# A fused attention and gated feed-forward kernel: three weight loads go to ScalarE's queue, scores wait for half of K, and the written-out order is replaced

## Chip, core and metric

The kernel runs on one core of a Trainium2 chip. The metric is the device time of one execution in microseconds (us). Before the change it is 263.43 us, the median of three runs (263.19 to 264.03).

## What is computed

From the reference, cut to what matters (one batch, 2048 tokens, width 512, 32 heads of 16, four segments of 512 tokens, feed-forward width 1792):

```python
q, k, v = x @ wq, x @ wk, x @ wv            # split into 32 heads, 4 segments
for s in range(4):
    p = softmax(q[s] @ k[s].T * scale + causal_mask)
    a_dot = p @ v[s]
    pq = phi(q[s])                           # t + 1 if t > 0 else exp(t)
    a_mem = (pq @ M) / (pq @ z + 1e-6)
    out[s] = g_head * a_mem + (1 - g_head) * a_dot
    M, z = M + phi(k[s]).T @ v[s], z + phi(k[s]).sum(rows)
a = concat(out) @ wo
b = (relu(x @ W_gate) * (x @ W_up)) @ W_down
result = g * a + (1 - g) * b                 # g = sigmoid(x . gate_w), one per token
```

## The kernel before

**Work.** Each segment's attention is done in four units of eight heads. A unit has four score groups (`qk`, line 634, eight matmuls each), each followed on ScalarE by one exponential of 128x2048 values from PSUM to SBUF (line 656), by masking on GpSimd (line 685), and, when all four are done, by the product with V (line 707). The score groups all write the same four PSUM banks, so a score group waits for the exponential of the one before it. Every second unit has a further group for the diagonal blocks (line 647). Between two score groups TensorE is given matmuls of 512 columns from other parts, here called fills: the projections of q, k and v (weights `wq_sb`, `wk_sb`, `wv_sb`), the two feed-forward projections (`wg_sb`, `wu_sb`) and the output (`wd_sb`, `wo_sb`). All go through `full`: as one matmul (line 476), or, when TensorE is in its column form already, as four quarter-width ones (line 480).

**After a projection.** Q is copied from PSUM by VectorE (line 567). K is copied to `ktr` (line 583), and then masked into `KT` in three pieces (line 586): the first serves score groups with `r = 0`, the second those with `r = 1`, the third the diagonal. `ktr` also goes through an exponential on ScalarE (line 546) and two VectorE steps to `pkT` (lines 541 and 542).

**Order.** Nothing is scheduled at run time. Every step is a task with an engine and with the tasks it depends on; `ORDER` lists the tasks' numbers in the order in which they are written out, and `UNITS` says which PSUM bank or buffer each takes. Each engine executes its own tasks in that order; the waits between engines come from the dependences.

**Loads.** Loads at the start stand in the code ahead of the plan. ScalarE's queue issues the second quarter of the first x rows (n1) and one row block of wq (q1), then ScalarE loads its table and copies two pieces of x. SyncE's queue issues, in this order: n0, q0, a transposed half of x, q2, q3, wk in two halves of rows, wv, the first 512 columns of W_gate (g0) and of W_up (u0), gate_w, beta, the next 512 columns of W_gate and W_up (g1, u1), the rest of the first x rows (n2), the transposed x of the second segment, and the remaining columns. In the built program every load adds to one of eight landing counters, taken in turn, and waits, before it is issued, until the earlier load on its counter has landed.

Of the kernel before, what the change touches and what calls it, by code (L numbers as in the profile page):

```python
# [9 lines left out]
ACT = mybir.ActivationFunctionType  # L10
# [83 lines left out]
"""  # L94

UNITS = (
    "456701237654305000122212611232212100100000100000000130110000003000300002301130200031220202"
    "14113320353207112630381119110d320b102a221c100102102200031022000121112200033220200104563012"
    "000003200000002201100000320002000020011312212203031113a32230207013430163028200b21350219122"
    "c303d0112011031320210001131302032220322331021456721030000023000000022011000002300020000310"  # L100
    "111220213112163223212b3012121530243008013a01390037612d201c00121201322100312122323022013100"
    "145631200000023000000023011000000000000007001131230220103122362025300b320220081234211a0239"
    "715d4027326c10011200110"
)


class Slot:


    def __init__(self, cands):  # L110
        self.cands, self.units, self.left = tuple(cands), (), 0

    @property
# [66 lines left out]
def kernel(  # L180
# [74 lines left out]
    def work():  # L255
        return plan.one("ps", range(7, -1, -1))


    LANDS = dict(n0=3470, n1=3600, q0=4500, q1=4550, x0=5600, q2=5900, q3=6400, ka=7700,
                 kb=9600, v=11000, g0=12500, u0=13800, gw=14800, be=15100, g1=16300, u1=17500,  # L260
                 n2=18500, x1=21500, g2=22800, u2=23900, g3=25000, u3=26100)

# [726 lines left out]
```

## Time and profile before

| | |
|---|---|
| median of three runs | 263.43 us |
| the profiled execution's own time | 263.58 us |
| its span | 261.9 us |
| TensorE clock granted | 1.0 throughout |
| TensorE matmul busy | 254.7 us (97%) |
| VectorE busy | 203.7 us (78%) |
| ScalarE busy | 183.2 us (70%) |
| GpSimd busy | 64.2 us (25%) |
| DMA, mean rate over the span | 75 GB/s |
| DMA, rate in the first six slices of 6.5 us | 193, 293, 292, 269, 221, 241 GB/s |

The span is what the profiler saw of the program; the profiled execution's time is 1.7 us longer. Engine rows are named PE (TensorE matmul), PEld (TensorE weight load), DVE (VectorE), ACT (ScalarE), POOL (GpSimd) and SP (SyncE); a q behind the name (SPq, ACTq) is that engine's issue of a load. L476 is line 476 of the kernel. A row of the timeline reads: start in us, duration in us, engine, line, operation, what is written from what, shapes, count, and in brackets the idle time of the engine just before it with what ended it. A row of the list of waits reads: who waited for whom, total us, times, longest. A row of the chain of waits reads: start, duration, what the chain ran through. A row by stretch reads: the stretch, its length, then busy us and count of PE, PEld, DVE, ACT and POOL, the TensorE clock, the busy share of the DMA engines, and GB/s.

### The profile page before, as it was taken

Reading aid. Unit: us, or ns where it says so; the run is one execution under the profiler, and the core shown is the slowest. Engines: PE = TensorE matmul, PEld = TensorE weight load, DVE = VectorE, ACT = ScalarE, POOL = GpSimd, SP = SyncE. Lnnn points to the kernel's source line nnn. Section 1 sums busy time; section 2 is a strip of 40 time slices with the busy share of each in tenths; the row PEclk is TensorE's granted clock in tenths of the full one; section 3 lists DMA queues with packets and bytes.
Section 4 is the critical chain, followed back from the end, with each engine's and each line's share of the span. In section 5 each row is a group of like instructions: output and inputs, shape, how many; then the busy total and the mean of one; then the engine's idle time right before and its main releaser. Section 6 shows DMA issues by size and latency. Waiting matters only on the chain.

```text
span 261.9 us, 8759 instructions
## 1 busy us (share of the span) xinstructions
PE 254.7 (97%) x3769; PEld 116.9 (45%) x3798; DVE 203.7 (78%) x472; ACT 183.2 (70%) x168; POOL 64.2 (25%) x168
## 2 busy tenths in 40 slices
PE   8899999999999999999999999999999999999995
PEld 3344434453444354544444444445444444445454
DVE  1899999888896756958989868858988678788622
ACT  2199998998877788787768576878486768972100
POOL 8023462313321223222112222122122232120000
PEclk9999999999999999999999999999999999999999
DMA  7999887021411202100210500140200100330011
GB/s 193 293 292 269 221 241 145 4 43 23 84 34 43 92 22 72 45 0 3 83 21 3 95 4 21 55 150 3 80 4 20 32 7 23 97 108 3 3 43 40
DMA packets 31581, 19.71 MB, mean 75 GB/s; under 512 B 16056, under 2 KB 30008, under 8 KB 31544
## 3 DMA queue, kind: packets, MB, share of 16 engines
q1 hardware_dynamic: 31128, 18.90, 27.1%
q8 instruction: 29, 0.48, 0.7%
q10 hardware_dynamic: 416, 0.26, 0.3%
q14 instruction: 8, 0.07, 0.1%
HBM read 13.21 MB, written 2.55 MB: 60 GB/s over the span
## 4 chain that ended last, share of the span: by engine, by line
PE 90%; DVE 5%; issue 1%; DMA 1%; SPq 1%; ACT 0%; DVEq 0%; ACTq 0%
PE ps L476 54%; PE ps L480 19%; PE ps L634 8%; PE ps L707 7%; DMA wq_sb<-in_A_wq_dram 1%; DVE ktr L583 1%; PE ps L647 1%; DVE KT L586 1%; PE ps L827 1%; SPq L304 1%; DVE QT L567 0%; PE ps L763 0%; DVE T L738 0%; DVE hT L877 0%; PE ps L803 0%
## 5 line engine op out<-in xcount | busy, mean ns | idle before, releaser
L656 ACT ACTIVATE E<-ps 128x2048 bf16<-128x2048 f32 x64 | 120.1, 1877 | 32.7 <-PE ps L634 22.5
L685 POOL TENSOR_SCALAR_AFFINE_SELECT E<-E 128x256 bf16<-128x256 bf16 x128 | 55.5, 458 | 170.3 <-ACT E L656 170.3
L877 DVE TENSOR_TENSOR hT<-ps,rgr 128x512 bf16<-128x512 f32 x56 | 37.8, 683 | 13.1 <-PE ps L476 8.4
L476 PE MATMUL ps<-xT,wu_sb 128*128 128x512 bf16 x163 | 45.6, 380 | 0.7 <-issue 0.5
L871 ACT ACTIVATE rgr<-ps 128x512 bf16<-128x512 f32 x56 | 32.6, 596 | 15.3 <-PE ps L480 8.2
L476 PE MATMUL ps<-wd_sb,hT 128*128 128x512 bf16 (+1 forms) x174 | 41.7, 354 | 0.6 <-issue 0.5
L476 PE MATMUL ps<-xT,wg_sb 128*128 128x512 bf16 x149 | 40.9, 380 | 0.3
L738 DVE STREAM_TRANSPOSE T<-ps 128x512 f32<-128x512 f32 x32 | 22.2, 705 | 6.7 <-PE ps L707 6.6
L634 PE MATMUL ps<-QT,KT 32*128 32x320 bf16 (+3 forms) x512 | 25.4, 273 | 0.3
L476 PEld LDWEIGHTS <-wu_sb 128*128 128x128 bf16 x170 | 15.3, 98 | 19.4 <-issue 3.0
L476 PEld LDWEIGHTS <-hT 128*128 128x128 bf16 x178 | 15.6, 98 | 17.6 <-issue 2.1
L903 DVE TENSOR_SCALAR osr<-ps,ngcol 128x512 bf16<-128x512 f32 (+2 forms) x18 | 12.3, 691 | 13.3 <-PE ps L480 9.1
L476 PEld LDWEIGHTS <-wg_sb 128*128 128x128 bf16 x156 | 14.3, 98 | 17.8 <-issue 2.1
L707 PE MATMUL ps<-E,Vp 128*17 128x320 bf16 (+3 forms) x512 | 19.4, 273 | 0.0
L634 PEld LDWEIGHTS <-KT 32*128 32x128 bf16 x512 | 7.6, 92 | 25.7 <-issue 24.6
L656 ACT ACTIVATE Em<-ps 128x2048 bf16<-128x2048 f32 x8 | 15.0, 1874 | 5.0 <-PE ps L647 5.0
L480 PE MATMUL ps<-xT,wg_sb 128*32 128x512 bf16 x272 | 17.8, 379 | 0.0
L476 PE MATMUL ps<-wv_sb,xT 128*128 128x512 bf16 x59 | 16.7, 380 | 0.8 <-DMA wv_sb<-in_A_wv_dram 0.6
L480 PE MATMUL ps<-wd_sb,hT 128*32 128x512 bf16 (+1 forms) x296 | 16.9, 359 | 0.0
L476 PE MATMUL ps<-xT,wq_sb 128*128 128x512 bf16 x57 | 15.8, 380 | 0.4 <-ACT xT L528 0.2
L476 PE MATMUL ps<-xT,wk_sb 128*128 128x512 bf16 x54 | 15.3, 379 | 0.2 <-issue 0.2
L480 PE MATMUL ps<-xT,wu_sb 128*32 128x512 bf16 x216 | 15.0, 379 | 0.0
(100 smaller groups left out, 293.1 us busy)
## 6 DMA issues: line engine op xcount, KB each, us to landing
out_dram<-osr SPq DMA_DIRECT2D x15, 128.0 KB
wd_sb<-in_B_W_down_dram SPq DMA_DIRECT2D x2, 896.0 KB
xn<-in_A_x_dram SPq DMA_DIRECT2D x3, 512.0 KB
cdr<-coefs SPq DMA_DIRECT2D x6, 256.0 KB
xn<-coefs SPq DMA_DIRECT2D x6, 256.0 KB
wg_sb<-in_B_W_gate_dram SPq DMA_DIRECT2D x2, 512.0 KB
wu_sb<-in_B_W_up_dram SPq DMA_DIRECT2D x2, 512.0 KB
wg_sb<-in_B_W_gate_dram SPq DMA_DIRECT2D x2, 384.0 KB
```

Source lines behind the costliest of these rows:

```text
L304: nc.sync.dma_start_transpose(out=xT[0][:, NC // 2:NC, :], in_=x[0:L, halves[1]])
L476: nc.tensor.matmul(out, lhsT=lhsT, rhs=rhs, start=start, stop=stop)
L480: nc.tensor.matmul(out[r], lhsT=lhsT[:, r], rhs=rhs, start=start, stop=stop, tile_position=(0, 32 * j))
L583: d = plan.add("DVE", 600, key - RQK, lambda: nc.vector.tensor_copy(ktr[ks.i][:], bank(sl)), [a], DVL + 40, need=[ks], frees=[sl])
L634: nc.tensor.matmul(ps[:, j * L + o:j * L + o + L - q], lhsT=KT[i][rows, kb, 3 * r:3 * r + 2].rearrange("p h q -> p (h q)"), rhs=QT[i][rows ...
L656: last_exp[0] = [plan.add("ACT", 66 + 4 * L / 1.2, key, lambda: nc.scalar.activation(dst, ps[:, 0:4 * L], ACT.Exp, scale=SCALE), [a] + war ...
L685: nc.gpsimd.affine_select(out=m[:, :, o:o + HP], in_=m[:, :, o:o + HP], compare_op=ALU.is_ge, fill=0.0, base=HP, pattern=[[0, 4], [1, HP]] ...
L707: nc.tensor.matmul(bank(sl)[32 * m:32 * m + HW, q:q + w], lhsT=(Vp[i] if n < 4 else Vm)[:, kb, r, 4 * c + j, 0:HW], rhs=rhs, start=(n == 0 ...
L738: done.append(plan.add("DVE", 633, key - RL, lambda r=r, sl=sl: nc.vector.transpose(T[ts.i][:, r], bank(sl)), [a] + done, 75 if r else 0, ...
L871: r = plan.add("ACT", 478, key - RL, lambda sl=gsl, rs=rs: nc.scalar.activation(rgr[rs.i][:], bank(sl), ACT.Relu), [g], ACL, frees=[gsl])
L877: nc.vector.tensor_tensor(hT[hs1.i][:], bank(sl), rgr[rs.i][:], ALU.mult)),
L903: nc.vector.tensor_scalar(osr[os.i][:, n0 - c0:n1 - c0], bank(sl)[:, 0:n1 - n0], ngcol[:, tt:tt + 1], None, ALU.mult)),
```

## The change

The second row half of wk, the second row half of wv, and u0 are no longer issued by SyncE ahead of the plan. They become three tasks on ScalarE that stand in its order after its two copies of x, chained one behind the other. SyncE keeps the first halves of wk and wv, then g0, gate_w, beta, g1, u1 and the rest as they were.

A score group now depends on its own masked piece of K (`prj["k", seg, c][r]`) instead of on all three.

`ORDER` and `UNITS` are new throughout, since the number of tasks and the assumed landing times (`LANDS`) changed. In the new order the first score group stands behind 30 wide matmuls from line 476 (34 before), the second to fifth behind two fewer than before, and from the eighth to the thirty-seventh group the counts are equal. On VectorE the product for the first `pkT` stands ahead of the third copy of K. Among SyncE's later loads wo now goes ahead of the transposed x of the third segment and of W_down.

```diff
-    got_k = [load_rows(nc.sync, wk_sb, A_wk, i, "k") for i in range(2)]
-    got_v = load_cols(nc.sync, wv_sb, A_wv, 0, D, "v")
-    load_gu(0)
+    got_k = [load_rows(nc.sync, wk_sb, A_wk, 0, "k")]
+    got_v = [load_rows(nc.sync, wv_sb, A_wv, 0, "v")]
+    got_g[0] = load_cols(nc.sync, wg_sb, B_W_gate, *FP[0], "g0")
     nc.sync.dma_start(out=gwb[:], in_=gate_w.partition_broadcast(P))
...
-        a = matmuls(key, xin(seg) + [got_v] + war, sl, [
+        a = matmuls(key, xin(seg) + got_v + war, sl, [
...
-            e = score(key, lambda r=r, k=k: qk(u, r, k), [prj["q", seg, c]] + prj["k", seg, c],
+            e = score(key, lambda r=r, k=k: qk(u, r, k), [prj["q", seg, c], prj["k", seg, c][r]],
                       Ef[:], eread.get(n - RE, []))
...
     got_x[0] = x0_tasks()
+
+    def rows(w, ap):
+        return lambda: nc.scalar.dma_start(out=w[:, 2:4, :],
+                                           in_=ap.rearrange("(c p) n -> p c n", p=P)[:, 2:4, :])
+    deps = got_x[0][0]
+    for got, emit, lat in (
+            (got_k, rows(wk_sb, A_wk), 2600), (got_v, rows(wv_sb, A_wv), 4300),
+            (got_u, lambda: nc.scalar.dma_start(
+                out=wu_sb[:, :, 0:FP[0][1]],
+                in_=B_W_up.rearrange("(c p) n -> p c n", p=P)[:, :, 0:FP[0][1]]), 6800)):
+        a = plan.add("ACT", 470, K(-8), emit, deps, lat)
+        if got is got_u:
+            got_u[0] = a
+        else:
+            got.append(a)
+        deps = [(a, 0.0)]
     load_late()
```

More of the change, by code (lines that the diff above doesn't have):

```diff
@@ L30 @@
 ORDER = """
[63 rows of a table removed]
[63 rows of a table added]
 """
 UNITS = (
[L97 to L103, printed above, removed]
+    "456701237654305000102222211131222123100000110000000120110000030000000002301100101021023210"
+    "24310332350007011621082209121d201a213b203c001112000130031110213231032112102032301145671320"
+    "000003200000002201100000130003000001011322201203031213b22132227303431061238021a30150029201"
+    "c000d1102011030212230021122211022320332323031245610320000031000000023011000002200010000200"
+    "11023131301222110b0235303311380114201a300611291207123d021c12000211122000102132223121323021"
+    "345632010000021000000023011000003300000000701122353021013021122026302b2233302a221411080117"
+    "105d610c223901101200110"
 )
@@ L256, in work @@
         return plan.one("ps", range(7, -1, -1))
-    LANDS = dict(n0=3470, n1=3600, q0=4500, q1=4550, x0=5600, q2=5900, q3=6400, ka=7700,
-                 kb=9600, v=11000, g0=12500, u0=13800, gw=14800, be=15100, g1=16300, u1=17500,
-                 n2=18500, x1=21500, g2=22800, u2=23900, g3=25000, u3=26100)
+    LANDS = dict(n0=3470, n1=3500, q0=4200, q1=4500, x0=5500, q2=6050, q3=6650, ka=7600,
+                 va=9800, g0=12600, gw=13800, be=14300, g1=15600, u1=17000, n2=18100, x1=21200,
+                 g2=22500, u2=23600, g3=24700, u3=25800)
     def arrival(name):
@@ L322 @@
     got_d, got_o = [], []
-    plan.add("SP", 22000, -1e9, None, xfer=4500.0)
+    plan.add("SP", 21000, -1e9, None, xfer=4500.0)
     def load_late():
```

126 rows, old and new, of the table ORDER are left out of this document.

## The prediction

> **What bounds the kernel now.** I read the page's busy times first, then the chain of waits, the list of waits in the first 40 us, the timeline of the opening, and the DMA rate by microsecond.
>
> ```profile
> PE 254.7 (97%) x3769; PEld 116.9 (45%) x3798; DVE 203.7 (78%) x472; ACT 183.2 (70%) x168; POOL 64.2 (25%) x168
> ```
>
> TensorE works 254.7 of 261.9 us. What a change of order and of loads can win lies in the few microseconds where TensorE does not work; the chain shows where they are:
>
> ```profile
> 3.19 3.19 DMA wq_sb<-in_A_wq_dram
> 6.43 3.64 PE ps L476 x16
> ...
> 12.91 0.40 PE ps L634 x8
> 13.31 2.26 PE ps L476 x10
> 15.57 0.33 PE ps L634 x8
> 15.90 2.69 PE ps L476 x12
> 18.60 0.33 PE ps L634 x8
> ```
>
> From 12.91 us on a score group (L634, eight matmuls) and the projections between two of them (L476) follow each other without a hole, and this goes on to 259 us. Ten fills between two scores make a period of 2.60 us (12.91 to 15.51 in the timeline), twelve make 3.02 us (15.51 to 18.53), so a 512-wide fill costs 0.216 us. Before 12.91 the list of waits has one TensorE wait that the change can reach:
>
> ```profile
> PE ps L476 <- DMA wv_sb<-in_A_wv_dram: 0.6, 1, 0.6
> ```
>
> From the end of the last wk matmul to the first wv matmul at 11.51 the hole in starts is 0.757 us more than the usual 0.216. That is the most that can be won here: 0.76 us, 0.3% of the time. (The short gap at 12.77 is a missing matmul record: six weight loads stand beside five matmuls.) The timeline shows ScalarE beside it:
>
> ```profile
> 4.03 0.65 ACT L528 CAST xT<-ps 128x256 bf16<-128x256 f32 x2 [0.88 <-PE ps L513]
> ...
> 10.82 1.23 ACT L546 ACTIVATE ex<-ktr 128x512 bf16<-128x512 bf16 x2 [6.14 <-DVE ktr L583]
> ...
> 13.37 1.88 ACT L656 ACTIVATE E<-ps 128x2048 bf16<-128x2048 f32 x1 [1.32 <-PE ps L634]
> ...
> 16.14 1.88 ACT L656 ACTIVATE E<-ps 128x2048 bf16<-128x2048 f32 x1
> ```
>
> ScalarE is free from 4.68 to 10.82 us, then does two exponentials of K (0.52 us apart) and the first score's exponential, 1.88 us, which the second score group waits for. From there ScalarE is over 90% busy up to 40 us, so a late start is not made up.
>
> The trace also records when the sixteen parts of each load report. The last parts: n0 3.31 us, n1 (ScalarE's queue) 3.51, q3 6.80, first half of wk 7.67, second half 8.40, wv 11.47, g0 (first part of W_gate) 12.90, u0 (first part of W_up) 14.26, gate_w 14.71. In KB landed since the start: 1280 at 7.67, 1536 at 8.40, 2048 at 11.47, 2560 at 12.90, 3072 at 14.26, 3200 at 14.71. I call this the landing curve.
>
> **The change, part by part.** *Three issues on ScalarE.* The two it has now took 0.48 and 0.53 us (0.80 to 1.84), and its table load starts only at 1.87: its stream is served in order. Three more cost 1.5 us, free in the idle stretch if nothing holds them. But the changed program's listing gives each load one of eight landing counters in turn, and a load waits until the earlier load on its counter has landed. SyncE's loads wait so too, and hold nothing else. On ScalarE the second half of wk waits for q3, that of wv for the first half of wv, and u0 for gate_w, which stands on SyncE's queue behind g0. Behind u0 stand the first exponential of K and all that follows.
>
> *Gate 1, second half of wk.* It starts at 6.85 (q3 at 6.80), not at 4.76 as on SyncE. TensorE does six wq, two wk and one wq matmul from 6.43, 9 x 0.216, and stands at 8.38. When does the half land? At best as n0, start to landing 2.50 us: 9.35. By the curve, with nothing of g0 ahead of it (1280 + 256 + 256 = 1792 KB), 9.93. If it takes turns with g0, of which some 100 KB are ahead, 1536 + 100 + 512 = 2148 KB, 11.75. After all of g0, 12.2. That the two queues are served side by side is seen at the start, where n0 and n1 land 0.2 us apart. I take 10.9, about midway between 9.93 and 11.75, because the slow parts of wv (9.19 to 11.47) need not fall on it. After it come 11 wq and wk matmuls and two of wv (2.8 us), the change of form (0.1), the first score and twelve fills (3.02): second score at landing + 5.93 = 16.83.
>
> *Gate 2, ScalarE.* gate_w is now behind 2176 KB at least (n, wq, x, half wk, half wv, g0, itself): 11.83 by the curve; with both second halves before it, 2688 KB, 13.25. I take 13.2, the second halves being issued by 9 us. Then the issue of u0 (0.05 + 0.5), two exponentials (1.0), the first score's (1.88) and 0.1: second score at landing + 3.55 = 16.75. On VectorE the product pkT, now ahead of the third copy of K, waits for the same first exponential; after it come 0.35, 0.27 and 0.61 us and then four W_gate fills, at landing + 3.4: just covered by gate 2. u0 itself then lands near 16.8 (as n1, 2.7 us, with 0.3 for its size), needed at 17.2: covered by 0.4 us, and a loss one for one past that.
>
> *What it is compared with.* Before the second to fifth scores the new order has two fills less (42 against 44 at the second), from the eighth on the same number. The point of the old run that answers is 15.51 - 2 x 0.216 = 15.08. The later gate, 16.83, is 1.75 us behind, and nothing later gives it back: TensorE has no hole after 13 us to fill. Bounds: gates at 9.93 and 11.83 give 15.86, +0.8; at 12.2 and 13.35 they give 18.13, +3.05; at the least row, 9.35, gate 1 gives +0.2.
>
> *Score waits for its own half of K.* The first score needed three masked pieces of K, done at 12.1, while TensorE was on wv until 12.9: the wait cost nothing. Now the first piece is due at landing + 2.3, TensorE at landing + 2.9: 0.6 us of cover.
>
> *SyncE.* Two issues leave it (0.47 and 0.51 us) and one is halved. Its loads up to u0 were all issued by 6.84, before their bytes had their turn, so this wins nothing. Of the reordered later loads W_down landed by 42.9 and is first used at 68.7, 26 us of cover. *Rest of the order.* 36 quarter matmuls (L480, 54 ns apart) become 9 whole ones of 216 ns: no difference. Changes of matmul form number 152 against 151, some 0.1 us each.
>
> The Trainium skill, "DMA: Bandwidth & Descriptors", section "Issuing engines are not separate DMA queues", says that loads of all engines run on the same sixteen DMA engines and that issuing from several saves only issue time. The landings above agree: wk was issued 2.9 us and u0 7.4 us before it landed, so issue time was not what they waited for. By that rule the split brings none of the rate that the second rival below needs, and I set its chance lower for it.
>
> The sum against the profiled execution: 263.58 + 1.75 = 265.3, of which 261.9 was the span and 1.7 lies around it. That execution is 0.15 above the median of 263.43; for the median I predict 265.2.
>
> **The rivals.** *A longer hold on ScalarE.* SyncE's later issues took much longer than 0.5 us when much was queued:
>
> ```profile
> 9.10 1.91 SPq L267 DMA_DIRECT2D wu_sb<-in_B_W_up_dram  x1
> ```
>
> If u0's issue takes 1.91 on ScalarE, gate 2 becomes 13.2 + 4.96 = 18.16, +3.1: 266.5. Against it: ScalarE's own queue has only two small loads before u0.
>
> *The two queues fill the idle DMA time (not slower).* The mean rate sagged where wv was under way:
>
> ```profile
> 8.00:9.00 1.00, 1.00 (x6) 0.44 (x5) 1.00 (x3) 0.00 (x0) 0.00 (x0) 1.00 0.71 219
> ...
> 11.00:12.00 1.00, 0.49 (x3) 0.25 (x4) 1.00 (x4) 1.00 (x2) 0.00 (x0) 1.00 1.03 365
> ```
>
> At 365 GB/s from 7.67 the 1152 KB up to gate_w (half wv, g0, gate_w, second half of wk) would be in by 10.9, and gate 2 (14.45) would not bind. Gate 1 decides: at its least of 9.35 the second score comes at 15.28, +0.2, the same time, 263.6. To be level it would have to land at 9.15, 2.3 us after its issue, when no load of the opening took less than 2.5; with every hold gone, -0.76 (262.7) is the end.
>
> *Only the first piece of the hold.* Both gates at their low curve values: 264.2, on the border of what can be measured.
>
> **How the numbers follow.** About 0.3%, 0.8 us, is what a measurement of this kernel can tell from no change. Both gates near the values taken (+0.9 to +2.6): 0.62. Longer hold or later landing (over +2.6): 0.17. Low curve values: 0.12, half of it counted as slower by over 0.3%. Idle DMA time filled: 0.09, of which 0.03 faster by more than 0.3% (all of the hole won, and a little of the run's own spread), the rest the same. So slower 0.62 + 0.17 + 0.06 = 0.85, same 0.12, faster 0.03. The range, 263.7 to 266.6, leaves out about 0.1 at either end.
>
> **What would show it.** Right: in the profile after, ScalarE's third new issue starts with gate_w's landing, near 13 us, with the first exponentials of K behind it near 14; TensorE waits for wk_sb from about 8.4 to 11; the second score starts near 16.8; no TensorE hole from 20 us on. Step by step wrong: first exponential of K before 12 us (gate 2 does not bind); wk_sb wait under 1 us (gate 1 sized wrongly); holes past 20 us (the loss is in the new order instead). The forecast is wrong if the second score group starts before 15.5 us.

## The result, and the profile after

The changed kernel takes 277.67 us (median of five, 275.0 to 278.45), the kernel before 263.43 (262.97 to 264.03) beside it: ratio 1.0525, 95% interval 1.0469 to 1.0580. The prediction was 265.2, with a range up to 266.6. The direction was right; the loss is 14.2 us instead of 1.75. The traced execution of the changed kernel took 277.82 us, with a span of 276.1 against 261.9.

The page first, busy times and the row of the granted TensorE clock in 40 slices (6.9 us each; 9 is full):

```profile
PE 260.3 (94%) x3742; PEld 119.4 (43%) x3771; DVE 204.5 (74%) x472; ACT 183.9 (67%) x168; POOL 62.5 (23%) x168
...
PEclk9868699999999999999999999999999999999999
```

TensorE is busy 5.6 us longer for the same work, and its clock row, which held 9 throughout before, has two dips, an 8 and a 6 in slices 2 and 3 and again in slices 4 and 5. So there are two losses: time in which TensorE stands still, and time in which it works slowly. The list of waits in the first 40 us gives the standstill (total us, times, longest):

```profile
PE ps L476 <- DMA wk_sb<-in_A_wk_dram: 5.4, 1, 5.4
PE ps L476 <- DMA wu_sb<-in_B_W_up_dram: 3.8, 1, 3.8
```

Before, the one wait of this kind was 0.6 us for wv; it is gone. Now TensorE waits once for the second half of wk and once for u0, two of the three loads that went to ScalarE. The rows by stretch give the slow work (length, busy us of PE, PEld, DVE, ACT, POOL, then the clock, the DMA share and GB/s):

```profile
10.00:20.00 10.00, 5.68 (x22) 2.02 (x24) 4.02 (x9) 1.42 (x3) 0.00 (x0) 0.66 1.13 229
20.00:30.00 10.00, 6.24 (x28) 2.27 (x28) 4.03 (x11) 5.31 (x6) 1.57 (x4) 0.79 1.24 234
```

A mean clock of 0.66 over 10 us, where it is either 1.0 or 0.5, is (1 - 0.66) x 10 / 0.5 = 6.8 us at half clock. The clock records put two such stretches of 6.83 us at 12.07 to 18.89 and at 25.72 to 32.55. They begin 3.3 and 2.9 us after TensorE stopped (8.76 and 22.82), while it still stands, and last into the work behind the hole. The timeline shows what led to it, and what it cost:

```profile
6.50 0.38 ACTq L928 DMA_DIRECT2D wk_sb<-in_A_wk_dram  x1
...
8.47 0.38 ACTq L928 DMA_DIRECT2D wv_sb<-in_A_wv_dram  x1
...
11.12 8.29 SPq L274 DMA_TRANSPOSE xT<-in_A_x_dram  x1
...
13.21 0.38 ACTq L933 DMA_DIRECT2D wu_sb<-in_B_W_up_dram  x1
...
14.16 1.03 PE L476 MATMUL ps<-xT,wk_sb 128*128 128x512 bf16 x2 [5.39 <-DMA wk_sb<-in_A_wk_dram]
...
15.41 3.61 PE L476 MATMUL ps<-xT,wk_sb 128*128 128x512 bf16 x8
...
15.95 0.63 ACT L546 ACTIVATE ex<-ktr 128x512 bf16<-128x512 bf16 x1 [10.93 <-DVE ktr L583]
...
22.42 0.40 PE L634 MATMUL ps<-QT,KT 32*128 32x448 bf16 x8
...
26.57 1.89 PE L476 MATMUL ps<-xT,wu_sb 128*128 128x512 bf16 x4 [3.76 <-DMA wu_sb<-in_B_W_up_dram]
```

The second half of wk is issued by ScalarE at 6.50, right behind q3's landing (6.48 in this trace), and lands at 14.11, 7.6 us later. u0 is issued at 13.21, right behind gate_w's landing (13.19), and lands at 26.53, 13.3 us later. Eight matmuls from 15.41 on take 3.61 us. The second score group starts at 22.42, where it started at 15.51 before.

The start of the score exponentials (L656) says when the loss is complete:

| exponential | before, us | after, us | later by |
|---|---|---|---|
| 1st | 13.37 | 19.84 | 6.47 |
| 2nd | 16.14 | 23.02 | 6.88 |
| 3rd | 18.98 | 32.47 | 13.49 |
| 8th | 33.14 | 47.32 | 14.18 |
| 72nd | 233.49 | 247.80 | 14.30 |

From the eighth on (equal work before it) the loss stays at 14.0 to 14.3 us up to the 37th. After that the two orders differ and it moves between 12.8 and 15.5, but at the last it is 14.30 again.

**Theory.** Loads of both queues are served about in their order of issue. The wait for q3's counter costs the second half of wk only some 1.7 us of issue time against SyncE (4.76 before), but in these SyncE has issued g0, gate_w and beta, and the half lands behind them. u0, issued at 13.21, falls beside the transposed x of the second segment. Each hole brings the clock to half for a while, which is paid a second time. **Rivals:** the new order itself is slower; ScalarE's queue gets only a small share of the DMA time whatever the time of issue; the half clock costs nothing that later waits don't take anyway.

### The profile page after: what moved, and what is told of

The parts are those of the page before. It is cut to its first block, busy times and chain, and to the rows that moved or that the text cites. A ratio compares the mean times of both kernels' runs of the same rounds, so it can differ in the third digit from the quotient of the medians.

```text
span 276.1 us, 8693 instructions
## 1 busy us (share of the span) xinstructions
PE 260.3 (94%) x3742; PEld 119.4 (43%) x3771; DVE 204.5 (74%) x472; ACT 183.9 (67%) x168; POOL 62.5 (23%) x168
## 3 DMA queue, kind: packets, MB, share of 16 engines
HBM read 13.21 MB, written 2.55 MB: 57 GB/s over the span
## 4 chain that ended last, share of the span: by engine, by line
PE 88%; DMA 7%; SPq 2%; issue 1%; ACT 0%; DVE 0%
PE ps L476 53%; PE ps L480 18%; PE ps L634 8%; PE ps L707 7%; DMA wu_sb<-in_B_W_up_dram 5%; DMA gwb<-in_gate_w_dram 3%; SPq L267 1%; PE ps L647 1%; PE ps L827 1%; SPq L304 0%; PE ps L803 0%; PE ps L763 0%; ACT rgr L871 0%; DVE osr L903 0%
## 5 line engine op out<-in xcount | busy, mean ns | idle before, releaser
L656 ACT ACTIVATE E<-ps 128x2048 bf16<-128x2048 f32 x64 | 120.1, 1877 | 34.1 <-PE ps L634 24.0
L685 POOL TENSOR_SCALAR_AFFINE_SELECT E<-E 128x256 bf16<-128x256 bf16 x128 | 53.8, 445 | 186.4 <-ACT E L656 186.3
L877 DVE TENSOR_TENSOR hT<-ps,rgr 128x512 bf16<-128x512 f32 x56 | 37.7, 684 | 21.5 <-PE ps L476 15.7
L476 PE MATMUL ps<-xT,wu_sb 128*128 128x512 bf16 x169 | 48.4, 386 | 4.9 <-DMA wu_sb<-in_B_W_up_dram 3.8
L476 PE MATMUL ps<-xT,wg_sb 128*128 128x512 bf16 x171 | 47.5, 389 | 0.4 <-issue 0.2
L476 PE MATMUL ps<-wd_sb,hT 128*128 128x512 bf16 (+1 forms) x160 | 37.4, 352 | 0.4 <-issue 0.3
L476 PEld LDWEIGHTS <-wu_sb 128*128 128x128 bf16 x180 | 16.4, 98 | 24.1 <-DMA wu_sb<-in_B_W_up_dram 4.0
L476 PEld LDWEIGHTS <-wg_sb 128*128 128x128 bf16 x174 | 16.7, 100 | 21.3 <-issue 3.4
L480 PE MATMUL ps<-wd_sb,hT 128*32 128x512 bf16 (+1 forms) x356 | 21.4, 362 | 0.0
L476 PEld LDWEIGHTS <-hT 128*128 128x128 bf16 x163 | 13.8, 98 | 15.9 <-issue 3.4
L476 PE MATMUL ps<-xT,wk_sb 128*128 128x512 bf16 x44 | 14.8, 437 | 5.6 <-DMA wk_sb<-in_A_wk_dram 5.4
L656 ACT ACTIVATE Em<-ps 128x2048 bf16<-128x2048 f32 x8 | 15.0, 1876 | 4.6 <-PE ps L647 4.5
L476 PE MATMUL ps<-xT,wq_sb 128*128 128x512 bf16 x59 | 16.4, 389 | 0.1
L546 ACT ACTIVATE ex<-ktr 128x512 bf16<-128x512 bf16 x12 | 7.5, 624 | 12.4 <-DVE ktr L583 12.4
L476 PE MATMUL ps<-wv_sb,xT 128*128 128x512 bf16 x53 | 15.6, 390 | 0.2 <-issue 0.2
L583 DVE CAST ktr<-ps 128x512 bf16<-128x512 f32 x16 | 10.9, 679 | 6.5 <-PE ps L476 6.2
```

What stands on the lines that cost most here:

```text
L476: nc.tensor.matmul(out, lhsT=lhsT, rhs=rhs, start=start, stop=stop)
L480: nc.tensor.matmul(out[r], lhsT=lhsT[:, r], rhs=rhs, start=start, stop=stop, tile_position=(0, 32 * j))
L546: return es, plan.add("ACT", 520, key + 500, lambda: nc.scalar.activation(ex1[es.i][:], src(), ACT.Exp), [a], ACL, need=[es])
L583: d = plan.add("DVE", 600, key - RQK, lambda: nc.vector.tensor_copy(ktr[ks.i][:], bank(sl)), [a], DVL + 40, need=[ks], frees=[sl])
L656: last_exp[0] = [plan.add("ACT", 66 + 4 * L / 1.2, key, lambda: nc.scalar.activation(dst, ps[:, 0:4 * L], ACT.Exp, scale=SCALE), [a] + war ...
L685: nc.gpsimd.affine_select(out=m[:, :, o:o + HP], in_=m[:, :, o:o + HP], compare_op=ALU.is_ge, fill=0.0, base=HP, pattern=[[0, 4], [1, HP]] ...
```

## The experiments

Each ran beside the kernel before, whose median was 263.65 to 263.98 us in these runs. In kernels with added lines the numbers of lines are a little higher (L476 is L479 in the first).

**1. All three loads back on SyncE**, with the new order and the half-K waits kept.

```diff
     got_k = [load_rows(nc.sync, wk_sb, A_wk, 0, "k")]
+    nc.sync.dma_start(out=wk_sb[:, 2:4, :], ...)
     got_v = [load_rows(nc.sync, wv_sb, A_wv, 0, "v")]
+    nc.sync.dma_start(out=wv_sb[:, 2:4, :], ...)
     got_g[0] = load_cols(nc.sync, wg_sb, B_W_gate, *FP[0], "g0")
+    nc.sync.dma_start(out=wu_sb[:, :, 0:FP[0][1]], ...)
...
-        a = plan.add("ACT", 470, K(-8), emit, deps, lat)
+        a = plan.add("ACT", 470, K(-8), None if got is got_k or got is got_v or got is got_u else emit, deps, lat)
```

> The changed kernel's order, units and half-K waits, but the three loads go back to SyncE's queue at the places they had before (wk, wv in two row halves each, u0 behind g0). Theory (the whole loss comes from the three loads on ScalarE): the second half of wk lands near 8.4 us, u0 near 14.3, TensorE has no hole above 0.8 us before 30 us, the granted clock is 1.0 throughout, and the time is 262.7 to 263.6 us. Rival (part of the loss is in the new order or in the half-K waits): the time stays above 264.5 us with the loads back at their old landings.

Measured: 264.28 us (264.14 to 264.88), ratio 1.0024 (1.0015 to 1.0034), clock 1.0 throughout. The second half of wk lands at 8.47, u0 at 14.07. So 277.7 - 264.3 = 13.4 of the 14.2 us are in the three loads. The time is between the two expectations: some 0.6 us belongs to the rest of the change (which of its parts, the order or the half-K waits, no run separates). Its list of waits shows holes that the old order did not have:

```profile
PE ps L479 <- DMA wg_sb<-in_B_W_gate_dram: 0.8, 1, 0.8
PE ps L479 <- DVE hT L880: 0.4, 1, 0.4
```

The second score group starts at 14.46, 0.62 us ahead of the point that the prediction compared with (15.08), and then the order asks for g1 at 16.26, which lands at 17.04. The lead is gone there, and by the eighth exponential this trace is 1.1 us behind the one of before.

**2. u0 alone back on SyncE**, behind beta; the halves of wk and wv stay on ScalarE.

```diff
     got_be = arrival("be")
+    nc.sync.dma_start(out=wu_sb[:, :, 0:FP[0][1]], ...)
...
-        a = plan.add("ACT", 470, K(-8), emit, deps, lat)
+        a = plan.add("ACT", 470, K(-8), None if got is got_u else emit, deps, lat)
```

> The changed kernel, but u0 alone goes back to SyncE (behind beta, ahead of g1); the second halves of wk and wv stay on ScalarE. Theory (two separate stalls, each paid twice: the hole itself and a stretch of half clock behind it): TensorE still waits some 5.4 us for wk_sb and the clock still falls once, near 12 us (2.4 us more); the wait for wu_sb (3.8 us) and the second stretch of half clock (3.0 us) go: 277.7 - 6.8 = 270.9 us. Rival (the loss after 20 us follows from the first stall alone, the late start of everything): a second hole and a second fall of the clock stay and the time stays above 275 us.

Measured: 270.86 us (270.25 to 271.69), ratio 1.0258 (1.0243 to 1.0273). One wait and one stretch of half clock are left, in the list of waits and the rows by stretch:

```profile
PE ps L477 <- DMA wk_sb<-in_A_wk_dram: 4.7, 1, 4.7
```
```profile
10.00:20.00 10.00, 6.26 (x23) 2.06 (x24) 4.45 (x11) 1.38 (x3) 0.00 (x0) 0.66 1.06 267
20.00:30.00 10.00, 10.00 (x66) 4.07 (x65) 8.13 (x27) 9.63 (x11) 2.66 (x6) 1.00 0.75 202
```

The two stalls are separate, and the second, u0's, is worth 277.7 - 270.9 = 6.8 us with its half clock. The stretch was not of one length in all four runs: two of them, without a trace, have a mean clock of 0.994 and not 0.987, which makes about 3 us at half clock instead of 6.8 (estimated as above, 0.006 x 269 / 0.5).

**3. Only u0 on ScalarE**, the halves of wk and wv back on SyncE (edits as in 1 and 2). Its landing counter is now that of the first half of wk.

> The changed kernel, but the second halves of wk and wv go back to SyncE; only u0 stays on ScalarE. Its landing counter is then that of the first half of wk (landed near 7.7 us), so it is issued near 7.7 us and not near 13.2. Theory (loads of both queues are served about in the order of issue, so it is the late issue that makes u0 late): u0 lands between 15 and 17 us, TensorE has at most 1 us of hole, the clock stays 1.0, 263.3 to 264.5 us. Rival (ScalarE's queue gets a small share while SyncE's is full, whatever the time of issue): u0 lands past 19 us, TensorE waits over 2 us for wu_sb, and the time is above 266 us.

Measured: 266.85 us (264.88 to 267.72), ratio 1.0097 (1.0068 to 1.0127), clock 1.0. The traced run is the 264.88: u0 issued at 7.27, landed at 15.67, hole 0.89 us. That is the theory's case for the landing and the hole; but no run lies within its 263.3 to 264.5 us, and four of the six took 266.7 to 267.7. Two further traces were taken to see that slower outcome.

> The version with u0 alone on ScalarE once more, for a second trace: six runs of it gave 264.9 and 265.2, and then 266.7 to 267.7 us, and only the first was traced (u0 issued at 7.27 with the landing of the first half of wk, ahead of the second columns of W_gate, issued by SyncE at 7.86; landed at 15.67; hole 0.89 us). Theory (order of issue is order of landing): where the first half of wk lands after some 7.85 us, u0's issue falls behind that load, u0 lands near 17.2 us, TensorE waits some 2.5 us for it, and the time is 266.6 to 267.7 us; where it lands earlier, the first trace repeats with 264.9 to 265.3 us. Rival (the spread comes from elsewhere): a time near 267 us with u0 landed before 16 us, or the other way round.

> A third trace of the version with u0 alone on ScalarE; the same two outcomes: issue of u0 before 7.85 us goes with a landing near 15.7 us and 264.9 to 265.3 us, issue behind the second columns of W_gate goes with a landing near 17.2 us and 266.6 to 267.7 us.

Measured: 265.18 and 265.29 us. u0 was issued at 7.45 and 7.44, ahead of g1 both times (7.84 and 7.83), and landed at 16.34 and 16.45, the holes being 1.1 and 1.7 us:

```profile
PE ps L478 <- DMA wu_sb<-in_B_W_up_dram: 1.1, 1, 1.1
```
```profile
PE ps L478 <- DMA wu_sb<-in_B_W_up_dram: 1.7, 1, 1.7
```

Issued near 7.4 instead of 13.2, u0 lands 10 us earlier from the same queue: against the rival of a starved queue. (The times agree with the expectation for an early issue; the landing near 15.7 that was to go with it came 0.7 us later.) The outcome at 267 us fell into no trace; that there u0 is issued behind g1 remains a supposition.

**4. TensorE kept busy in both waits** of the changed kernel: `keep_warm(b, n)` adds n matmuls of constants (128x512) into PSUM bank b.

```diff
+    extra = [(got_k[1], 1, 22), (got_u[0], 4, 26)]
     for t in order:
+        for a, b, n in extra:
+            if t.eng == "PE" and a is not None and any(d is a for d, _ in t.deps):
+                keep_warm(b, n)
...
```

> The changed kernel with idle work added on TensorE and nothing left out: 22 matmuls of constants into a PSUM bank not yet in use where it waits for the second half of wk, and 26 where it waits for u0. Theory (the granted clock falls because TensorE stands still, and costs 2.4 us behind the first hole and 3.0 behind the second): the clock stays 1.0; the loads land when they landed, so what the first stretch gave back is waited for at u0, and the second stretch is won: about 274.7 us, 3.0 less than 277.7. Rival (the halved clock stands in the records but costs nothing, or it falls for another reason than the holes): 277.7 us or a little more.

Measured: 275.40 us (274.45 to 276.51), ratio 1.0439 (1.0416 to 1.0462), 2.3 us under the changed kernel and 0.7 short of the expectation, clock 1.0 throughout; in its trace both awaited loads landed later than in the changed kernel, the half of wk by 1.4 us and u0 by 1.15. Its timeline, the same eight wk matmuls that took 3.61 us:

```profile
15.52 0.61 PE L476 MATMUL ps<-xT,wk_sb 128*128 128x512 bf16 x2 [1.84 <-DMA wk_sb<-in_A_wk_dram]
...
16.18 1.89 PE L476 MATMUL ps<-xT,wk_sb 128*128 128x512 bf16 x8
...
21.46 0.40 PE L634 MATMUL ps<-QT,KT 32*128 32x448 bf16 x8
```

The half clock follows from TensorE standing still, and it costs. From the landing of the second half of wk (15.47) to the second score group 5.99 us, against 22.42 - 14.11 = 8.31 in the changed kernel. From u0's landing (27.68) to the end of the span it is 247.1 us, against 249.6. So the first stretch cost 2.3 us and the second 2.5. A pause of 1.84 us, which was left where the 22 matmuls ran out, did not bring the clock down.

**5. The transposed x of the second segment issued last**, behind the last columns of W_up; the three loads stay on ScalarE.

```diff
-    load_xT(1)
...
     load_gu(3)
+    load_xT(1)
```

> The changed kernel with all three loads on ScalarE, but the transposed x of the second segment is issued by SyncE behind the last columns of W_up instead of ahead of the third columns of W_gate. Theory (u0, issued at 13.2 us, lands at 26.5 only because it meets the 256-byte pieces of that transposed load and the pause before them): u0 lands between 18 and 21 us, before TensorE asks for it at 22.8; the wait for wu_sb and the second stretch of half clock go, 277.7 - 6.8 = about 270.9 us. Rival (ScalarE's queue is starved by whatever SyncE has queued): u0 still lands past 24 us and the time stays above 275 us.

Measured: 272.39 us (271.55 to 273.64), ratio 1.0321 (1.0285 to 1.0357). u0, issued at 11.97, lands at 20.77; TensorE does not wait for it, and the clock is back at 1.0 from 20 us on. So u0's 26.5 us came in the main from the company it was issued into: it took 8.8 us from issue to landing and not 13.3 (it was also issued 1.24 us earlier, as gate_w landed at 11.96). Of the 1.5 us above the expectation 0.9 lie in the first stall: q3 landed at 6.95 here, the half of wk was issued at 6.97 and landed at 15.02, not 14.11. The rest is not accounted for.

**6. The second half of wk issued early by ScalarE**, in the kernel of experiment 1.

```diff
-    nc.sync.dma_start(out=wk_sb[:, 2:4, :], ...)
+    late = sb([P, P], BF16, "late")
+    nc.scalar.copy(late[:], xn[:, 0, 0:P])
+    nc.scalar.dma_start(out=wk_sb[:, 2:4, :], ...)
```

> The version with all loads on SyncE in the changed order (264.3 us), but the second half of wk is issued by ScalarE, right behind a small copy from the first x rows that is added so that the issue comes near 3.8 us, with no wait for a landing counter of q3. Theory (it is the time of issue and not the queue that made this half land at 14.1 us): it lands between 7 and 9 us, TensorE does not wait over 0.7 us for wk_sb, the clock stays 1.0, and the time is 264.0 to 265.0 us. Rival (ScalarE's queue has a small share while SyncE's is full): it lands at 11 us or later, TensorE waits over 2.5 us, and the time is above 266.5 us.

Measured: 264.81 us (264.46 to 265.27), ratio 1.0032 (1.0021 to 1.0044), clock 1.0. The timeline and the list of waits:

```profile
3.26 0.41 ACTq L310 DMA_DIRECT2D wk_sb<-in_A_wk_dram  x1
```
```profile
PE ps L481 <- DMA wq_sb<-in_A_wq_dram: 0.5, 1, 0.5
```

Issued at 3.26 the half lands at 7.93, from the same queue. TensorE waits for a part of wq instead: the half was issued just behind q2 (3.21) and ahead of q3 (3.83), and these two now land at 7.41 and 8.11 (6.04 and 6.69 in experiment 1). What the half gains by its early issue, the loads beside it lose. And a load that SyncE issues as late takes as long: its u0 in the kernel before, issued at 6.34, landed at 14.26; the half, issued by ScalarE at 6.50 in the changed kernel, at 14.11.

**7. TensorE kept busy in the one wait left in experiment 2** (22 matmuls, as in 4).

> The version with u0 alone back on SyncE (270.9 us; one hole of some 5 us before wk_sb and one stretch of half clock), with 22 matmuls of constants added where TensorE waits for the second half of wk; nothing is left out. Theory (a stretch of half clock of 6.8 us costs the half of the 4.7 us that TensorE works in it): clock 1.0, about 268.5 us, 2.4 less. Rival (the half clock costs nothing that later waits do not take anyway): 270.9 us.

Measured: 270.72 us (269.5 to 273.41), ratio 1.0268 (1.0221 to 1.0315). By the time alone the rival holds. The trace shows why the time could not tell: the clock is 1.0 throughout, but q3 landed at 6.76 instead of 6.45, the half of wk was issued at 6.78 instead of 6.47, and landed at 15.65 instead of 13.70. From that landing to the end of the span it is 253.8 us, against 256.3 in experiment 2: 2.5 us are won by the clock, and 1.95 lost to a later landing. The price of the half clock is shown by this difference within the traces, not by the median. In one of the four runs, the one of 273.41 us, the mean clock was 0.994: there it fell for a while in spite of the 22 matmuls.

Side by side, the five traces in which the half of wk waits for q3, with the next large load that SyncE issues:

| experiment | issue of the half | landing | next large load: issue, landing |
|---|---|---|---|
| 2 | 6.47 | 13.70 | u0: 6.81, 15.93 |
| the change | 6.50 | 14.11 | g1: 6.82, 15.66 |
| 7 | 6.78 | 15.65 | u0: 6.79, 15.86 |
| 4 | 6.80 | 15.47 | g1: 6.81, 15.67 |
| 5 | 6.97 | 15.02 | g1: 6.81, 15.91 |

Issued 0.3 us ahead of that load, the half lands 1.6 and 2.2 us ahead of it; issued beside it, 0.2 us ahead; issued 0.16 us behind it (experiment 5), still 0.9 us ahead, with half as many bytes. So the order of issue is the order of landing only roughly. A shift of 0.3 us in q3's landing, which changes from run to run, moves the half's landing by up to 2 us.

The packet records of the changed kernel show how the half moved. From the half's issue to 10.2 us only SyncE's queue (q1) moves packets, those of loads issued before; then both queues do, ScalarE's (q10) too. The view of the DMA queues gives packets, MB and their share, first for 6.5 to 10.2 us and then for 10 to 11 us:

```profile
q1 hardware_dynamic: 985, 0.95, 88.4%
```
```profile
q1 hardware_dynamic: 171, 0.11, 53.7%
q10 hardware_dynamic: 78, 0.08, 22.3%
```

The half's first packet starts at 10.24, 3.74 us behind its issue; the same lag is 2.6 to 4.2 us in experiments 2, 4, 5 and 7. From there it shares the DMA engines with gate_w, beta and g1, and the rate of both queues together is low at first:

```profile
10.00:11.00 1.00, 0.00 (x0) 0.00 (x0) 0.00 (x0) 0.00 (x0) 0.00 (x0) 1.00 0.76 188
11.00:12.00 1.00, 0.00 (x0) 0.00 (x0) 0.00 (x0) 0.00 (x0) 0.00 (x0) 1.00 0.91 253
```

In the kernel before the same two microseconds moved 313 and 365 GB/s. Why the half moves nothing for so long, and why the rate sags here, no run shows.

**8. g1 ahead of beta and gate_w**, in the kernel of experiment 1, to take away the new order's hole there.

```diff
+    nc.sync.dma_start(out=wg_sb[:, :, FP[1][0]:FP[1][1]], ...)
+    nc.sync.dma_start(out=betab[:], ...)
     nc.sync.dma_start(out=gwb[:], ...)
...
-    nc.sync.dma_start(out=betab[:], ...)
...
-    load_gu(1)
+    nc.sync.dma_start(out=wu_sb[:, :, FP[1][0]:FP[1][1]], ...)
```

> The version with all loads on SyncE in the changed order (264.3 us; there TensorE waits 0.83 us for the second columns of W_gate, which land at 17.04), with these columns issued ahead of beta and gate_w instead of behind them. Theory (in the opening the order of issue is the order of landing, and the new order is held up by this one load alone): they land near 15.7 us, that hole goes, and the second score still starts near 14.5 us, 0.6 ahead of the old order: 263.2 to 263.6 us, level with or a little under the kernel before. Rival (another load is late next, or the order itself is slower further on): 264 us or more.

Measured: 264.78 us (264.34 to 265.45), ratio 1.0027 (1.0013 to 1.0042), no better than experiment 1. g1 lands at 15.27 and its hole is gone, but the second score starts at 15.40 and not near 14.5. In this trace wk lands later (first half 8.68, not 7.82; second 9.41, not 8.47), and TensorE waits for it:

```profile
PE ps L482 <- DMA wk_sb<-in_A_wk_dram: 0.8, 1, 0.8
```

This hole lies ahead of the edited loads. Why the median shows no gain is not settled by this one trace.

**9. The kernel before, with wv in two row halves on SyncE**, nothing else.

```diff
-    got_v = load_cols(nc.sync, wv_sb, A_wv, 0, D, "v")
+    nc.sync.dma_start(out=wv_sb[:, 0:2, :], ...)
+    nc.sync.dma_start(out=wv_sb[:, 2:4, :], ...)
+    got_v = arrival("v")
```

> The kernel before, with its own order, loads all on SyncE, and one part of the change alone: wv is loaded in two row halves, so that its first matmuls wait for the first half only. Theory (the 0.76 us hole before wv is what can be won in the opening, and the first half lands near 9.8 us, the second near 11.2): the hole closes to about 0.1 us; of the 0.65 us won some 0.2 is lost again at the first columns of W_gate, which land at 12.7 to 12.9 and are then wanted at 12.6: 0.4 to 0.6 us under the kernel before. Rival (what is won is waited for at the next loads, since the rate of the opening is the bound): level with the kernel before within 0.2 us.

Measured: 263.81 us (263.36 to 264.38), ratio 1.0005 (0.9989 to 1.0020): level. The wait for wv is gone from the list. The score groups run 0.26 us ahead up to 108 us, where 0.48 us is lost in a product with V (L709); the rest of the 0.76 was lost in the wq matmuls, 16 of them in each trace, which end with the first wk matmul at 8.17 in the kernel before and at 8.67 here:

```profile
4.49 3.84 PE L476 MATMUL ps<-xT,wq_sb 128*128 128x512 bf16 x16 [0.16 <-ACT xT L528]
4.56 4.28 PE L478 MATMUL ps<-xT,wq_sb 128*128 128x512 bf16 x16
```

The clock records say why. In every trace TensorE begins at half clock (its first seven matmuls, of constants, take 2.8 us); the records put the rise to 1.0 at 3.75 us in the kernel before and at 5.92 here, and the wq matmuls up to 5.81 stand 0.42 us apart instead of 0.216. Over all traces the rise lies between 3.75 and 6.76 us, so single traces of the opening differ by some tenths of a microsecond for this reason alone. The hole that the change aims at can be closed, but over twelve runs no gain can be told from none.

## Why the prediction was right or wrong

Three steps failed: the landing of the second half of wk (10.9 taken, 14.11 measured), the landing of u0 (16.8 taken, 26.53 measured), and the clock, which the sum left at full speed (it cost 2.3 and 2.5 us). One by one:

*Gate 2, the issue: right.* gate_w's landing was put at 13.2 and came at 13.19; u0's issue follows at 13.21. It took 0.38 us and not 0.5. The landing was right by luck in part: 13.2 was taken because both second halves were to be in ahead of gate_w, and they landed behind it, at 14.11 and 16.68; what made up for that is probably the low rate from 10 to 12 us. Nor does gate 2 set the second score: the exponential of K at 15.95 waits for VectorE's copy of K, thus for gate 1.

*Gate 1, the landing of the half: the term that was too small.* 10.9 was taken, 12.2 was the upper bound, 14.11 came. The step that failed is "I take 10.9, about midway between 9.93 and 11.75": the half was to share the engines with g0 from its issue on, and for 3.74 us it moved nothing. Then it shared them with gate_w, beta and g1 and landed behind g0 (11.10), gate_w (13.19) and beta (13.69). That is 3.2 of the loss. The upper bound, "after all of g0", left out gate_w and beta, which SyncE issues ahead of it too (5.80 and 6.35; 136 KB, about 0.4 us by the landing curve), the part of g1 that moved beside the half, and the low rate. The Trainium skill, "DMA: Bandwidth & Descriptors", section "Queues, rings and completion order", says that each DMA engine alternates between the queues for which it has work, packet by packet. The estimate of 11.75 applied this from the issue on; the trace shows packets of both queues side by side only from 10.24 us on, and all five landings (13.70 to 15.65) are later than 11.75.

*Landing to second score, 5.93 us: right at full clock.* Experiment 4 measures 5.99. In the changed kernel it was 8.31, and the 2.4 us more than the forecast are the half clock, a term that the prediction put at nothing without a word. Its own wait, 8.4 to 10.9 us, is a hole of 2.5 us, and no run shows what the clock does at that length; at its upper bound of 12.2 the hole is 3.8, as long as the one at u0 that brought the clock down. 16.83 + 3.2 + 2.4 = 22.4 is the second score's measured start.

*u0, "covered by 0.4 us, and a loss one for one past that": wrong in the landing and in the price.* It was to land near 16.8 "as n1, 2.7 us" behind its issue, the value of a load that met empty queues. It took 13.3 us, because it met SyncE's pieces of the transposed x (experiment 5: 20.77 without them; experiment 3: 8.4 to 9.0 us from issue to landing when issued at 7.4). The loss was the hole, 3.76, and the clock behind it, 2.5 by experiment 4 up to the end. The loads issued beside u0 had no place in the sum.

*The sum.* Second score 22.42 - 15.08 = 7.3; the hole 3.8; the second half clock 2.5 to 3.0: 13.6 to 14.1, where the spans differ by 14.2.

*Score waits, rest of the order: small, but not nothing.* Taken as free; experiment 1 puts them at 0.24% together, 0.6 us. The prediction compared numbers of fills and not what each fill waits for: in experiment 1 g1 is asked for at 16.26 and lands at 17.04. (W_down is first used at 62.9 us, not at 68.7: 20 us of cover and not 26, which changes nothing.)

*The rivals.* The longer hold on ScalarE did not happen. The idle DMA time was not filled. What the Trainium skill says in "DMA: Bandwidth & Descriptors", section "Issuing engines are not separate DMA queues", that a second issuing engine saves only issue time, agrees with experiment 6: the early half on ScalarE's queue lands at 7.93, and the time is no better than with SyncE.

## What to carry to other kernels

Ask of a load that is moved to another engine when it will be issued there, and what the other queues have issued by then: its bytes wait for most of that, and a wait of under 2 us on a landing counter became 5.7 us of landing. Price a TensorE hole of the lengths seen here (3.8 us and more) at more than its length: the work behind it ran at half clock for 4.7 and 6.0 us in the changed kernel, up to the end of the stretch, and lost 2.3 and 2.5. Where an upper bound is far above the value taken, look for what would make it worse still before calling it a bound.

## What the runs showed of the hardware

- In holes of 3.76, 4.72, 5.17 and 5.39 us the clock fell to half each time; in pauses up to 1.84 us (experiment 4) it did not. A stretch lasted 6.83 us in all three traces that have one and cost 2.3 to 2.5 us. In each of these traces the clock changes only at steps of 6.83 us from its first rise (5.24, 12.07, 18.89, 25.72 and 32.55 us in the changed kernel), so the time from TensorE's stop to the fall is no constant. Mean clocks of 0.981 (one run of the changed kernel, 275.0 us) and 0.994 (two runs of experiment 2) make 10.4 us (instead of 13.7) and 3.2 us at half clock by the same estimate as above, so in runs without a trace there seem to be stretches of half that length. The Trainium skill, "TensorE: Matmul & The Clock Gate", section "HAM oscillation — how this bites in real kernels", warns of TensorE gaps over about 3.4 us; these traces agree: 3.76 us brings the clock down, 1.84 does not.
- While the issue of a transposed load was under way on SyncE (11.12 to 19.41 us in the changed kernel), almost nothing moved between 17.0 and 19.0 us by the packet records (43 and 24 GB/s). From 19.0 to 24.5 us u0 shared the DMA engines with its 256-byte pieces, and it landed at 26.53.
